# O and dQ of a grouped-query attention step from 64x256 instead of 32x128 matmul blocks

## The chip, the core and the metric

The kernel runs on one NeuronCore of a Trainium2 chip. The time is the device time of one execution in microseconds. A core has TensorE (PE: matmuls and transposes, which write PSUM), VectorE (DVE), ScalarE (ACT) and GpSimd (POOL) for elementwise work, and SyncE (SP), on whose queue this kernel issues all its transfers between SBUF and the main memory. Each engine works through its own instructions in order. A matmul takes a stationary operand, loaded by an instruction of its own (PEld in the profile), and streams a moving operand past it, column by column. The array can be split into tiles of fewer stationary columns that work side by side, each writing its own PSUM partitions. GpSimd does not take part in emptying PSUM in this kernel; VectorE and ScalarE do that.

## What is computed

Attention of 4 query positions for 32 query heads over 2048 keys in 4 key heads, for 32 batches with head size 128, and the gradients for q, k and v. Cut to what matters:

```python
def _fwd_reference(q, k, v):            # q (32, 32, 4, 128), k and v (32, 4, 2048, 128)
    k = jnp.repeat(k, rep, axis=1)      # rep = 8 query heads share one key head
    v = jnp.repeat(v, rep, axis=1)
    scores = jnp.einsum("bhqd,bhkd->bhqk", q, k) * scale
    p = _softmax(scores, axis=-1)
    return jnp.einsum("bhqk,bhkd->bhqd", p, v)

_out, _vjp = jax.vjp(_f, q, k, v)
_grads = _vjp(grad_out)                 # dq, dk, dv
```

For one batch, the 8 query heads times 4 positions of one key head are 32 rows, so the four key heads fill the 128 partitions: rows 32h to 32h+31 belong to key head h. With E the unnormalised softmax numerators (128 rows, 2048 keys), r the reciprocal of their row sums and G the output's gradient, the kernel makes

- O = r E V and dQ = r scale dS K, in which each group of 32 rows is multiplied by its own head's V or K;
- delta = the row sums of O times G, dS = E (G V^T - delta);
- dV = E^T (r G) and dK = dS^T (r scale Q).

## The kernel before

K and V of a batch come as two rows of SBUF each, one for two heads. Twenty such rows ("slots") hold loads and results alike: a result row is gathered in a slot and stored from there. The row for heads 2 and 3 of dV carries O behind its 4096 columns, that of dK carries dQ; the loaded rows of K carry q and the output's gradient in the same place.

The instructions stand in an order written out by hand. `PLAN` is one long text in which four characters are one unit: a letter for the kind of unit (`NAMES`, lines 23 to 26), its part, the engine, PSUM bank or slot that it uses, and a tile number. `emit` (line 214) turns a unit into instructions. The framework only adds the waits that the data and the buffers need, so all engines follow the order of this text.

The units of the change, by letter: `p`/`q` transpose E and empty PSUM; `r` (O) and `y` (DQ) are the products in question, in two halves each (lines 279 to 289); `s` (Oe) and `z` (DQe) scale them from PSUM into the result row (lines 290 to 296); `t` (DL) makes delta (lines 297 to 300); `u` (DP) and `v` (DS) are G V^T and dS in two halves; `A` and `C` are the matmuls of dV and dK, `B` and `D` empty them; `m`, `n` and `o` are three small GpSimd instructions (r G, r scale Q, r scale); `E` and `F` store dV and dK; `a` and `b` load K and V.

In a product of O, the stationary operand is a 128x32 piece of transposed E: 128 keys, the 32 rows of head h. The moving operand is 128 keys by 128 columns of V of the same head. Four such matmuls, one for each head, stand in four tiles of 32 stationary columns and write PSUM partitions 32h to 32h+31, columns 0 to 127 of one bank. Eight groups of four make one half, so O has 64 matmuls in a batch and dQ as many. dQ of one batch is made while the next batch's O is in work: in the order, O of batch b is followed by the two halves of dQ of batch b-1.

The order of one later batch around the change, with the units named in the text:

```
r020r1-0 s0D0 t0D0 o0-0 A640B6A0 A760B7D0 y030 C500D5A0 y1-0 z0D0 F180 u040 v0D0 ...
```

Delta follows directly on O's scaling, then come two parts of dV, dQ's two halves with a part of dK between them, dQ's scaling, the store of dK's second row with dQ in it, and then DP and dS, which reads delta.

A load or a store waits for its data, for its slot and for the transfer that last used its completion semaphore; all wait in SP's one queue.

Of the kernel before, what the change touches and what calls it, by code (L numbers as in the profile page):

```python
# [10 lines left out]
BF16 = mybir.dt.bfloat16  # L11
ACT = mybir.ActivationFunctionType
ALU = mybir.AluOpType

P = 128
NH = 4
ROW = 2 * 16 * P
# [36 lines left out]
    "f3D0A260B2A0E0c0u100v1D0g732h7A0e627f6A0n0-0C040D0D0C160D1A0C300D3D0a1g0g634h6A0g226h2A0i041i1-0j0D0C220D2A0g300"
    "h3A0e410f4A0w120x1A0g131h1D0k0A0g403h4D0g015h0D0C420D4D0w001x0A0l0D0e012f0A0C640D6A0F0i0C760D7D0e703f7A0e514p020"
    "q0A0f5D0b160p131q1D0m0-0A340B3A0A060B0D0A100B1A0a040r020r1-0s0D0t0D0o0-0A640B6A0A760B7D0y030C500D5A0y1-0z0D0F130"
    "u041v0D0g520h5A0A560B5A0E150b0e0A400B4D0e231f2A0e125f1A0c040d0D0e356f3D0A260B2A0E020u100v1D0g731h7A0e627f6A0n0-0"
    "C040D0D0C160D1A0C300D3D0a1b0g635h6A0g226h2A0i040i1-0j0D0C220D2A0g300h3A0e411f4A0w121x1A0g132h1D0k0A0g403h4D0g014"
    "h0D0C420D4D0w000x0A0l0D0e012f0A0C640D6A0F000C760D7D0e705f7A0e516p020q0A0f5D0b1a0p131q1D0m0-0A340B3A0A060B0D0A100"
    "B1A0a030r020r1-0s0D0t0D0o0-0A640B6A0A760B7D0y030C500D5A0y1-0z0D0F170u040v0D0g520h5A0A560B5A0E1i0b0f0A400B4D0e230"  # L60
    "f2A0e123f1A0c040d0D0e354f3D0A260B2A0E0c0u100v1D0g732h7A0e627f6A0n0-0C040D0D0C160D1A0C300D3D0a190g634h6A0g226h2A0"
    "i041i1-0j0D0C220D2A0g300h3A0e410f4A0w120x1A0g131h1D0k0A0g403h4D0g015h0D0C420D4D0w001x0A0l0D0e012f0A0C640D6A0F0h0"
    "C760D7D0e703f7A0e514p020q0A0f5D0b150p131q1D0m0-0A340B3A0A060B0D0A100B1A0a070r020r1-0s0D0t0D0o0-0A640B6A0A760B7D0"
    "y030C500D5A0y1-0z0D0F1j0u041v0D0g520h5A0A560B5A0E100b060A400B4D0e231f2A0e125f1A0c040d0D0e356f3D0A260B2A0E020u100"
    "v1D0g731h7A0e627f6A0n0-0C040D0D0C160D1A0C300D3D0a1e0g635h6A0g226h2A0i040i1-0j0D0C220D2A0g300h3A0e411f4A0w121x1A0"
    "g132h1D0k0A0g403h4D0g014h0D0C420D4D0w000x0A0l0D0e012f0A0C640D6A0F010C760D7D0e705f7A0e516p020q0A0f5D0b1i0p131q1D0"
    "m0-0A340B3A0A060B0D0A100B1A0a0j0r020r1-0s0D0t0D0o0-0A640B6A0A760B7D0y030C500D5A0y1-0z0D0F180u040v0D0g520h5A0A560"
# [3 lines left out]
    "t0D0o0-0A640B6A0A760B7D0y030C500D5A0y1-0z0D0F1g0u041v0D0g520h5A0A560B5A0E110b050A400B4D0e231f2A0e125f1A0c040d0D0"  # L71
    "e356f3D0A260B2A0E020u100v1D0g731h7A0e627f6A0n0-0C040D0D0C160D1A0C300D3D0a160g635h6A0g226h2A0i040i1-0j0D0C220D2A0"
    "g300h3A0e411f4A0w121x1A0g132h1D0k0A0g403h4D0g014h0D0C420D4D0w000x0A0l0D0e012f0A0C640D6A0F040C760D7D0e705f7A0e516"
    "p020q0A0f5D0b1h0p131q1D0m0-0A340B3A0A060B0D0A100B1A0a0g0r020r1-0s0D0t0D0o0-0A640B6A0A760B7D0y030C500D5A0y1-0z0D0"
    "F1b0u040v0D0g520h5A0A560B5A0E1d0b0i0A400B4D0e230f2A0e123f1A0c040d0D0e354f3D0A260B2A0E0c0u100v1D0g732h7A0e627f6A0"
    "n0-0C040D0D0C160D1A0C300D3D0a1a0g634h6A0g226h2A0i041i1-0j0D0C220D2A0g300h3A0e410f4A0w120x1A0g131h1D0k0A0g403h4D0"
    "g015h0D0C420D4D0w001x0A0l0D0e012f0A0C640D6A0F030C760D7D0e703f7A0e514p020q0A0f5D0b110p131q1D0m0-0A340B3A0A060B0D0"
    "A100B1A0a0b0r020r1-0s0D0t0D0o0-0A640B6A0A760B7D0y030C500D5A0y1-0z0D0F190u041v0D0g520h5A0A560B5A0E140b000A400B4D0"
    "e231f2A0e125f1A0c040d0D0e356f3D0A260B2A0E020u100v1D0g731h7A0e627f6A0n0-0C040D0D0C160D1A0C300D3D0a150g635h6A0g226"
    "h2A0i040i1-0j0D0C220D2A0g300h3A0e411f4A0w121x1A0g132h1D0k0A0g403h4D0g014h0D0C420D4D0w000x0A0l0D0e012f0A0C640D6A0"  # L80
    "F070C760D7D0e705f7A0e516p020q0A0f5D0b1d0p131q1D0m0-0A340B3A0A060B0D0A100B1A0a090r020r1-0s0D0t0D0o0-0A640B6A0A760"
    "B7D0y030C500D5A0y1-0z0D0F1e0u040v0D0g520h5A0A560B5A0E130b0h0A400B4D0e230f2A0e123f1A0c040d0D0e354f3D0A260B2A0E0c0"
    "u100v1D0g732h7A0e627f6A0n0-0C040D0D0C160D1A0C300D3D0a1i0g634h6A0g226h2A0i041i1-0j0D0C220D2A0g300h3A0e410f4A0w120"
    "x1A0g131h1D0k0A0g403h4D0g015h0D0C420D4D0w001x0A0l0D0e012f0A0C640D6A0F0f0C760D7D0e703f7A0e514p020q0A0f5D0b140p131"
    "q1D0m0-0A340B3A0A060B0D0A100B1A0a0e0r020r1-0s0D0t0D0o0-0A640B6A0A760B7D0y030C500D5A0y1-0z0D0F1j0u041v0D0g520h5A0"
# [3 lines left out]
    "s0D0t0D0o0-0A640B6A0A760B7D0y030C500D5A0y1-0z0D0F180u040v0D0g520h5A0A560B5A0E1f0b0d0A400B4D0e230f2A0e123f1A0c040"  # L89
    "d0D0e354f3D0A260B2A0E0c0u100v1D0g732h7A0e627f6A0n0-0C040D0D0C160D1A0C300D3D0a1h0g634h6A0g226h2A0i041i1-0j0D0C220"  # L90
    "D2A0g300h3A0e410f4A0w120x1A0g131h1D0k0A0g403h4D0g015h0D0C420D4D0w001x0A0l0D0e012f0A0C640D6A0F0a0C760D7D0e703f7A0"
    "e514p020q0A0f5D0b170p131q1D0m0-0A340B3A0A060B0D0A100B1A0a080r020r1-0s0D0t0D0o0-0A640B6A0A760B7D0y030C500D5A0y1-0"
    "z0D0F1g0u041v0D0g520h5A0A560B5A0E160b040A400B4D0e231f2A0e125f1A0c040d0D0e356f3D0A260B2A0E020u100v1D0g731h7A0e627"
    "f6A0n0-0C040D0D0C160D1A0C300D3D0a110g635h6A0g226h2A0i040i1-0j0D0C220D2A0g300h3A0e411f4A0w121x1A0g132h1D0k0A0g403"
    "h4D0g014h0D0C420D4D0w000x0A0l0D0e012f0A0C640D6A0F050C760D7D0e705f7A0e516p020q0A0f5D0b1f0p131q1D0m0-0A340B3A0A060"
    "B0D0A100B1A0a0g0r020r1-0s0D0t0D0o0-0A640B6A0A760B7D0y030C500D5A0y1-0z0D0F1b0u040v0D0g520h5A0A560B5A0E1a0b030A400"
    "B4D0e230f2A0e123f1A0c040d0D0e354f3D0A260B2A0E0c0u100v1D0g732h7A0e627f6A0n0-0C040D0D0C160D1A0C300D3D0a1d0g634h6A0"
    "g226h2A0i041i1-0j0D0C220D2A0g300h3A0e410f4A0w120x1A0g131h1D0k0A0g403h4D0g015h0D0C420D4D0w001x0A0l0D0e012f0A0C640"
    "D6A0F090C760D7D0e703f7A0e514p020q0A0f5D0b160p131q1D0m0-0A340B3A0A060B0D0A100B1A0a0b0r020r1-0s0D0t0D0o0-0A640B6A0"
    "A760B7D0y030C500D5A0y1-0z0D0F1i0u041v0D0g520h5A0A560B5A0E150b070A400B4D0e231f2A0e125f1A0c040d0D0e356f3D0A260B2A0"  # L100
# [6 lines left out]
    "r1-0s0D0t0D0o0-0A640B6A0A760B7D0y030C500D5A0y1-0z0D0F1j0u041v0D0g520h5A0A560B5A0E100b060A400B4D0e231f2A0e125f1A0"  # L107
    "c040d0D0e356f3D0A260B2A0E020u100v1D0g731h7A0e627f6A0n0-0C040D0D0C160D1A0C300D3D0a170g635h6A0g226h2A0i040i1-0j0D0"
    "C220D2A0g300h3A0e411f4A0w121x1A0g132h1D0k0A0g403h4D0g014h0D0C420D4D0w000x0A0l0D0e012f0A0C640D6A0F010C760D7D0e705"
    "f7A0e516p020q0A0f5D0b190p131q1D0m0-0A340B3A0A060B0D0A100B1A0a0j0r020r1-0s0D0t0D0o0-0A640B6A0A760B7D0y030C500D5A0"  # L110
    "y1-0z0D0F180u040v0D0g520h5A0A560B5A0E1h0b0a0A400B4D0e230f2A0e123f1A0c040d0D0e354f3D0A260B2A0E0c0u100v1D0g732h7A0"
    "e627f6A0n0-0C040D0D0C160D1A0C300D3D0a1f0g634h6A0g226h2A0i041i1-0j0D0C220D2A0g300h3A0e410f4A0w120x1A0g131h1D0k0A0"
    "g403h4D0g015h0D0C420D4D0w001x0A0l0D0e012f0A0C640D6A0F0d0C760D7D0e703f7A0e514p020q0A0f5D0b100p131q1D0m0-0A340B3A0"
    "A060B0D0A100B1A0a080r020r1-0s0D0t0D0o0-0A640B6A0A760B7D0y030C500D5A0y1-0z0D0F1g0u041v0D0g520h5A0A560B5A0E110b050"
    "A400B4D0e231f2A0e125f1A0c040d0D0e356f3D0A260B2A0E020u100v1D0g731h7A0e627f6A0n0-0C040D0D0C160D1A0C300D3D0a160g635"
    "h6A0g226h2A0i040i1-0j0D0C220D2A0g300h3A0e411f4A0w121x1A0g132h1D0k0A0g403h4D0g014h0D0C420D4D0w000x0A0l0D0e012f0A0"
    "C640D6A0F040C760D7D0e705f7A0e516p020q0A0f5D0b1h0p131q1D0m0-0A340B3A0A060B0D0A100B1A0a0g0r020r1-0s0D0t0D0o0-0A640"
    "B6A0A760B7D0y030C500D5A0y1-0z0D0F1b0u040v0D0g520h5A0A560B5A0E1d0b090A400B4D0e230f2A0e123f1A0c040d0D0e354f3D0A260"
    "B2A0E0c0u100v1D0g732h7A0e627f6A0n0-0C040D0D0C160D1A0C300D3D0a1a0g634h6A0g226h2A0i041i1-0j0D0C220D2A0g300h3A0e410"
    "f4A0w120x1A0g131h1D0k0A0g403h4D0g015h0D0C420D4D0w001x0A0l0D0e012f0A0C640D6A0F030C760D7D0e703f7A0e514p020q0A0f5D0"  # L120
    "b110p131q1D0m0-0A340B3A0A060B0D0A100B1A0a0b0r020r1-0s0D0t0D0o0-0A640B6A0A760B7D0y030C500D5A0y1-0z0D0F1i0u041v0D0"
# [3 lines left out]
    "r020r1-0s0D0t0D0o0-0A640B6A0A760B7D0y030C500D5A0y1-0z0D0F1e0u040v0D0g520h5A0A560B5A0E130b0h0A400B4D0e230f2A0e123"  # L125
    "f1A0c040d0D0e354f3D0A260B2A0E0c0u100v1D0g732h7A0e627f6A0n0-0C040D0D0C160D1A0C300D3D0a190g634h6A0g226h2A0i041i1-0"
    "j0D0C220D2A0g300h3A0e410f4A0w120x1A0g131h1D0k0A0g403h4D0g015h0D0C420D4D0w001x0A0l0D0e012f0A0C640D6A0F0f0C760D7D0"
    "e703f7A0e514p020q0A0f5D0b140p131q1D0m0-0A340B3A0A060B0D0A100B1A0a0e0r020r1-0s0D0t0D0o0-0A640B6A0A760B7D0y030C500"
    "D5A0y1-0z0D0F1j0u041v0D0g520h5A0A560B5A0E170b010A400B4D0e231f2A0e125f1A0c040d0D0e356f3D0A260B2A0E020u100v1D0g731"
    "h7A0e627f6A0n0-0C040D0D0C160D1A0C300D3D0a100g635h6A0g226h2A0i040i1-0j0D0C220D2A0g300h3A0e411f4A0w121x1A0g132h1D0"  # L130
    "k0A0g403h4D0g014h0D0C420D4D0w000x0A0l0D0e012f0A0C640D6A0F060C760D7D0e705f7A0e516p020q0A0f5D0b130p131q1D0m0-0A340"
    "B3A0A060B0D0A100B1A0a0j0r020r1-0o0-0s0D0t0D0A640B6A0A760B7D0y030C500D5A0y1-0z0D0F180u040v0D0g520h5A0A560B5A0E1f0"
    "b0d0A400B4D0e230f2A0e123f1A0c040d0D0e354f3D0A260B2A0E0c0u100v1D0g732h7A0e627f6A0n0-0C040D0D0C160D1A0C300D3D0a1h0"
    "g634h6A0g226h2A0i041i1-0j0D0C220D2A0g300h3A0e410f4A0w120x1A0g131h1D0k0A0g403h4D0g015h0D0C420D4D0w001x0A0l0D0e012"
    "f0A0C640D6A0F0a0C760D7D0e703f7A0e514p020q0A0f5D0p131q1D0b170m0-0A340B3A0A060B0D0A100B1A0r020r1-0s0D0t0D0o0-0A640"
    "B6A0A760B7D0y030C500D5A0y1-0z0D0F1g0u041v0D0g520h5A0A560B5A0E160b040A400B4D0e231f2A0e125f1A0c040d0D0e356f3D0A260"
    "B2A0E020u100v1D0g731h7A0e627f6A0n0-0C040D0D0C160D1A0C300D3D0g635h6A0g226h2A0i040i1-0j0D0C220D2A0g300h3A0e411f4A0"
    "w121x1A0g132h1D0k0A0g403h4D0g014h0D0C420D4D0w000x0A0l0D0e012f0A0C640D6A0F050C760D7D0e705f7A0e516p020q0A0f5D0p131"
    "q1D0m0-0A340B3A0A060B0D0A100B1A0r020r1-0s0D0t0D0o0-0A640B6A0A760B7D0y030C500D5A0y1-0z0D0F1b0u040v0D0g520h5A0A560"
    "B5A0E180A400B4D0e230f2A0e123f1A0c040d0D0e354f3D0A260B2A0E010u100v1D0g732h7A0e627f6A0n0-0C040D0D0C160D1A0C300D3D0"  # L140
    "g634h6A0g226h2A0i041i1-0j0D0C220D2A0g300h3A0w110x1A0g121h1A0k0A0g433h4D0g005h0D0C420D4D0w011x0A0l0D0C640D6A0F0f0"
    "C760D7D0p000q0A0p111q1D0m0-0A320B3A0A040B0D0A160B1A0r000r1-0s0D0t0D0o0-0A620B6A0A740B7D0y010C560D5A0y1-0z0D0F1c0"
    "u021v0D0g500h5A0A440A560B5A0E130B4D0A200B2A0E0a0u120v1D0n0-0C060D0D0C140D1A0C300D3A0C220D2A0w141x1A0C400D4D0w050"
# [17 lines left out]
def kernel(  # L161
# [11 lines left out]
    nc = tc.nc  # L173
# [14 lines left out]
    junk = const_pool.tile([P, D], BF16, name="junk")  # L188
# [13 lines left out]
    def bank(u, n=1):  # L202
        return psum[:, QW * int(u.where):QW * (int(u.where) + n)]
# [10 lines left out]
    def emit(u):  # L214
        b, name, i = u.b, u.name, u.part
        t = T[b]
        if name in ("LK", "LV"):
            x = slots[int(u.where, 36)]
            for h in range(2):
                t[name[1], 2 * i + h] = x[:, Sk * h:Sk * h + Sk]  # L220
            if name == "LK":
                t["q" if i == 0 else "go"] = x[:, ROW:LONG]
# [56 lines left out]
        elif name in ("O", "DQ"):  # L279
            if i == 0:  # L280
                t[name] = bank(u)[:, 0:D]
            xt, x = ("ET", "V") if name == "O" else ("DT", "K")
            left = t[xt, i][:].rearrange("p (j q e) -> p j q e", q=P, e=2)
            for c in range(8):
                j, odd = divmod(c, 2)
                for h, r in enumerate(rows):
                    right = t[x, h].rearrange("p (j d e) -> p j d e", d=D, e=2)
                    nc.tensor.matmul(t[name][r, :], lhsT=left[:, j, r, odd], rhs=right[:, 4 * i + j, :, odd],  # L288
                                     start=(i == 0 and c == 0), stop=(i == 1 and c == 7), tile_position=(0, 32 * h))
        elif name in ("Oe", "DQe"):  # L290
            x, by, to = ("o", "rinv", "DV") if name == "Oe" else ("dq", "rs", "DK")
            t[x] = t[to, "out", 1][:, ROW:LONG]
            if u.where == "A":
                nc.scalar.activation(out=t[x], in_=t[name[:-1]], func=ACT.Copy, scale=t[by][:])
            else:
                nc.vector.tensor_scalar(out=t[x], in0=t[name[:-1]], scalar1=t[by][:], scalar2=None, op0=ALU.mult)  # L296
        elif name == "DL":
            t["dl"] = sm_pool.tile([P, 1], FP32, name="delta")
            nc.vector.tensor_tensor_reduce(out=junk[:], in0=t["o"], in1=t["go"], scale=1.0, scalar=0.0,
                                           op0=ALU.mult, op1=ALU.add, accum_out=t["dl"][:])  # L300
        elif name == "DS":
# [60 lines left out]
```

## Time and profile before

| | us |
|---|---|
| three runs | 672.08, 670.65, 673.27 |
| median | 672.08 |
| span of the profiled execution | 671.1 |
| ACT busy in it | 569.6 |
| DVE busy in it | 572.0 |
| O's matmuls (L288, reading transposed E), busy | 36.1 |
| dQ's matmuls (L288, reading transposed dS), busy | 43.5 |
| L296, two of 128x128 a batch: mean | 0.34 and 0.35 |

The profile is of one execution. A page of it gives the busy time of each engine, the span in 40 slices with the share of time in which the transfers' sixteen engines were busy, the chain of work that ended last, and groups of equal instructions. A row of a timeline has the start and the length in us, the engine, the line of the kernel, the operation, and what it writes from what; a number in brackets is the time for which the engine had been idle before it, with what ended that. A row of a table of stretches has the stretch, its length, the busy time of each engine with the number of its instructions, the granted clock of TensorE as a share of the full one, the transfers' busy share and their rate. The busy time of matmuls that run side by side, or follow each other in the pipeline, is counted once, and each one's own length has the way through the array in it, so the pace of matmuls is read from the starts.

### The profile page before, as it was taken

What the parts mean: (1) busy time and instruction counts of PE and PEld (TensorE: products, weight loads), DVE (VectorE), ACT (ScalarE), POOL (GpSimd) and SP (SyncE); (2) the same over time, 40 slices, a digit from 0 to 9 for tenths busy, and PEclk for the clock granted to TensorE, in tenths of its full rate; (3) what the DMA queues carried; (4) which work ended last, traced back from release to release, by engine and by line L of the source; (5) the groups of instructions that cost most, each with busy time, mean ns of one, the idle gap of its engine ahead of it and who ended that gap; (6) DMA issues with size and microseconds to landing.
All of it is one profiled execution on the core that took longest, in us unless ns stands there. A gap on an engine that the chain in (4) does not pass through costs nothing.

```text
span 671.1 us, 20678 instructions
## 1 busy us (share of the span) xinstructions
PE 607.9 (91%) x8768; PEld 401.4 (60%) x8768; DVE 572.0 (85%) x736; ACT 569.6 (85%) x802; POOL 39.0 (6%) x102
## 2 busy tenths in 40 slices
PE   6998999999998999988998989988999989898993
PEld 5665566666665666655655655655655666565651
DVE  1988799999997999988888989887888979896994
ACT  4997899999997999888888989887888979886894
POOL 0000000000000000000000000000000000000000
PEclk9999999999998999999999999998999989998997
DMA  9999999999999999999999999999999999999867
GB/s 354 417 424 423 419 381 423 423 423 423 423 426 424 424 423 424 424 425 426 414 420 425 413 417 421 414 422 424 396 388 408 417 424 424 404 421 423 347 258 322
DMA packets 37533, 273.97 MB, mean 408 GB/s; under 512 B 4160, under 2 KB 4160, under 8 KB 5184
## 3 DMA queue, kind: packets, MB, share of 16 engines
q1 hardware_dynamic: 37440, 272.65, 98.2%
q8 instruction: 69, 1.13, 0.6%
q14 instruction: 24, 0.20, 0.1%
HBM read 136.31 MB, written 136.31 MB: 406 GB/s over the span
## 4 chain that ended last, share of the span: by engine, by line
DMA 50%; PE 37%; DVE 4%; ACT 4%; issue 3%; SPq 0%; POOL 0%; DVEq 0%; ACTq 0%; POOLq 0%
DMA row<-in_k_dram 50%; PE psum L241 19%; PE psum L310 8%; PE psum L288 5%; PE psum L255 5%; ACT row L316 3%; DVE vt_sb L209 2%; DVE ds_sb L303 1%; DVE row L316 0%; DVE e_sb L260 0%; ACT e_sb L264 0%; PE psum L230 0%; SPq L226 0%; ACT dt_sb L207 0%; DVE row L296 0%
## 5 line engine op out<-in xcount | busy, mean ns | idle before, releaser
L241 PE MATMUL psum<-ident,row 128*128 128x128 f32 x2048 | 290.1, 284 | 28.4 <-DMA row<-in_k_dram 21.5
L316 ACT CAST row<-psum 128x1024 bf16<-128x1024 f32 x292 | 289.2, 1023 | 30.9 <-PE psum L310 29.1
L241 PEld LDWEIGHTS psum<-ident,row 128*128 128x128 f32 x2048 | 224.7, 143 | 94.8 <-issue 32.0
L316 DVE CAST row<-psum 128x1024 bf16<-128x1024 f32 x220 | 264.9, 1217 | 5.7 <-PE psum L310 2.9
L207 ACT COPY kt_sb<-psum 128x512 f32<-128x512 f32 x190 | 110.2, 598 | 20.6 <-PE psum L241 20.4
L207 ACT COPY vt_sb<-psum 128x512 f32<-128x512 f32 x160 | 92.0, 602 | 35.3 <-PE psum L241 34.6
L303 DVE SCALAR_TENSOR_TENSOR ds_sb<-psum,delta,e_sb 128x1024 bf16<-128x1024 f32 x64 | 82.1, 1283 | 13.4 <-PE psum L255 9.0
L310 PE MATMUL psum<-ds_sb,qp_sb 32*128 32x512 bf16 x512 | 76.9, 383 | 3.4 <-ACT row L316 1.0
L260 DVE TENSOR_SCALAR_CACHE_REDUCE e_sb<-psum 128x2048 bf16<-128x2048 f32 x32 | 73.3, 2292 | 5.7 <-PE psum L255 5.7
L310 PE MATMUL psum<-e_sb,dop_sb 32*128 32x512 bf16 x512 | 68.8, 388 | 2.5 <-issue 1.0
L209 DVE COPY kt_sb<-psum 128x1024 bf16<-128x1024 bf16 x66 | 45.0, 685 | 28.4 <-PE psum L241 27.8
L209 DVE COPY vt_sb<-psum 128x1024 bf16<-128x1024 bf16 x96 | 60.7, 684 | 10.0 <-PE psum L241 9.8
L264 ACT ACTIVATE e_sb<-psum,m 128x2048 bf16<-128x2048 f32 x32 | 64.0, 2001 | 0.2 <-DVE e_sb L260 0.2
L271 POOL TENSOR_SCALAR dop_sb<-row,rinv 128x128 bf16<-128x128 bf16 x32 | 19.3, 603 | 605.3 <-DVE rinv L268 530.3
L241 PE MATMUL psum<-ident,ds_sb 128*128 128x128 f32 x256 | 41.8, 286 | 9.6 <-DVE vt_sb L209 7.0
L288 PE MATMUL psum<-row,dt_sb 128*32 128x128 bf16 x2048 | 43.5, 222 | 6.2 <-issue 5.6
L310 PEld LDWEIGHTS <-qp_sb 32*128 32x128 bf16 x512 | 19.4, 91 | 46.1 <-issue 42.6
L255 PE MATMUL psum<-vt_sb,qdt_sb 128*32 128x512 bf16 x512 | 40.7, 388 | 4.6 <-issue 4.5
L288 PEld LDWEIGHTS <-dt_sb 128*32 128x32 bf16 x2048 | 30.8, 95 | 22.0 <-issue 21.1
L241 PEld LDWEIGHTS psum<-ident,ds_sb 128*128 128x128 f32 x256 | 26.9, 140 | 27.2 <-DVE vt_sb L209 16.4
L207 ACT COPY dt_sb<-psum 128x512 f32<-128x512 f32 x63 | 38.4, 611 | 1.0 <-PE psum L241 0.9
L288 PEld LDWEIGHTS <-et_sb 128*32 128x32 bf16 x2048 | 30.4, 95 | 13.8 <-ACT et_sb L207 11.3
(29 smaller groups left out, 310.1 us busy)
## 6 DMA issues: line engine op xcount, KB each, us to landing
out_dram<-row SPq DMA_DIRECT2D x64, 1056.0 KB, 20.1
out_dram<-row SPq DMA_DIRECT2D x64, 1024.0 KB, 20.4
row<-in_k_dram SPq DMA_DIRECT2D x62, 1056.0 KB, 18.1
row<-in_v_dram SPq DMA_DIRECT2D x62, 1024.0 KB, 20.5
row<-in_v_dram SPq DMA_DIRECT2D x4, 512.0 KB, 9.4
row<-in_k_dram SPq DMA_DIRECT2D x2, 544.0 KB, 5.3
row<-in_k_dram SPq DMA_DIRECT2D x2, 512.0 KB, 4.4
```

What stands on the lines that cost most here:

```text
L207: nc.scalar.copy(out=out.bitcast(FP32), in_=in_)
L209: nc.vector.tensor_copy(out=out, in_=in_.bitcast(BF16))
L241: nc.tensor.transpose(out=ps[:, P * j:P * j + P], in_=src[:, 4 * half + j, :], identity=ident32[:])
L255: nc.tensor.matmul(out[r, QW * w:QW * w + QW], lhsT=t["qdt"][:, P * side + 32 * h:P * side + 32 * h + 32], rhs=t[x, NH * i + h][:, QW * w: ...
L260: nc.vector.tensor_scalar(out=t["e"][:], in0=t["S"], scalar1=-scale, scalar2=None, op0=ALU.mult, op1=ALU.min, accum_out=t["m"][:])
L264: nc.scalar.activation(out=t["e"][:], in_=t["S"], func=ACT.Exp, bias=t["m"][:], scale=scale, accum_out=t["l"][:])
L271: nc.gpsimd.tensor_scalar(out=t["dop"][:], in0=t["go"], scalar1=t["rinv"][:], scalar2=None, op0=ALU.mult)
L288: nc.tensor.matmul(t[name][r, :], lhsT=left[:, j, r, odd], rhs=right[:, 4 * i + j, :, odd], start=(i == 0 and c == 0), stop=(i == 1 and c ...
L303: nc.vector.scalar_tensor_tensor(out=t["ds"][:, w], in0=t["DP", i], scalar=t["dl"][:], in1=t["e"][:, w], op0=ALU.subtract, op1=ALU.mult)
L310: nc.tensor.matmul(acc[:, QW * (h % 2):QW * (h % 2) + QW], lhsT=t[still][rows[h], :], rhs=t[moving][rows[h], QW * i:QW * i + QW], start=Tr ...
L316: copy(out=heads_of(t[name[:2], "out", g])[:, :, QW * i:QW * i + QW], in_=t[name[:2], i, g].rearrange("p (h c) -> p h c", h=2))
```

## The change

O and dQ are made for two heads at a time. The stationary operand is 128x64, the rows of heads 2g and 2g+1; the moving operand is 128 keys by 256 columns, the same keys and columns of V or K of both heads, which lie in one row of SBUF. Two such matmuls stand in two tiles of 64 stationary columns. Of the 64x256 block that each makes, the two 32x128 blocks on the diagonal are the result; the other two, rows of one head times the other head's V or K, are not used. A half of O or dQ is 16 matmuls instead of 32, so a batch has 64 instead of 128 for both, and the PSUM block is 128x256.

VectorE scales the whole 128x256 block into one SBUF tile, `both`, which has one buffer, and GpSimd copies the four diagonal blocks from there to the result row. In the last batch VectorE scales the four blocks directly into the row. The tile `junk`, into which delta's instruction wrote products that nobody reads, is gone; that output goes into `both` as well. In the order, delta (`t`) is moved from behind O's scaling to behind the first half of DP (`u`), in every batch. Nothing else in the order changes.

```diff
-    ... r020r1-0s0D0t0D0o0-0A640B6A0A760B7D0y030C500D5A0y1-0z0D0F180u040v0D0 ...
+    ... r020r1-0s0D0o0-0A640B6A0A760B7D0y030C500D5A0y1-0z0D0F180u040t0D0v0D0 ...
...
-    junk = const_pool.tile([P, D], BF16, name="junk")
...
+            t[name[1], "pair", i] = x[:, 0:ROW]
...
-                t[name] = bank(u)[:, 0:D]
+                t[name] = bank(u)[:, 0:2 * D]
...
-                for h, r in enumerate(rows):
-                    right = t[x, h].rearrange("p (j d e) -> p j d e", d=D, e=2)
-                    nc.tensor.matmul(t[name][r, :], lhsT=left[:, j, r, odd], rhs=right[:, 4 * i + j, :, odd],
-                                     start=(i == 0 and c == 0), stop=(i == 1 and c == 7), tile_position=(0, 32 * h))
+                for g in range(2):
+                    r = slice(64 * g, 64 * g + 64)
+                    right = t[x, "pair", g].rearrange("p (h j d e) -> p h j d e", h=2, d=D, e=2)
+                    nc.tensor.matmul(t[name][r, :], lhsT=left[:, j, r, odd], rhs=right[:, :, 4 * i + j, :, odd],
+                                     start=(i == 0 and c == 0), stop=(i == 1 and c == 7), tile_position=(0, 64 * g))
...
-            if u.where == "A":
-                nc.scalar.activation(out=t[x], in_=t[name[:-1]], func=ACT.Copy, scale=t[by][:])
+            mine = [(r, slice(D * (h % 2), D * (h % 2) + D)) for h, r in enumerate(rows)]
+            both = sm_pool.tile([P, 2 * D], BF16, name="both", bufs=1)
+            if b == B - 1:
+                for r, c in mine:
+                    nc.vector.tensor_scalar(out=t[x][r, :], in0=t[name[:-1]][r, c], scalar1=t[by][r, :], scalar2=None,
+                                            op0=ALU.mult)
             else:
-                nc.vector.tensor_scalar(out=t[x], in0=t[name[:-1]], scalar1=t[by][:], scalar2=None, op0=ALU.mult)
+                nc.vector.tensor_scalar(out=both[:], in0=t[name[:-1]], scalar1=t[by][:], scalar2=None, op0=ALU.mult)
+                for r, c in mine:
+                    nc.gpsimd.tensor_copy(out=t[x][r, :], in_=both[r, c])
         elif name == "DL":
+            spare = sm_pool.tile([P, 2 * D], BF16, name="both", bufs=1)
             t["dl"] = sm_pool.tile([P, 1], FP32, name="delta")
-            nc.vector.tensor_tensor_reduce(out=junk[:], in0=t["o"], in1=t["go"], scale=1.0, scalar=0.0,
+            nc.vector.tensor_tensor_reduce(out=spare[:, 0:D], in0=t["o"], in1=t["go"], scale=1.0, scalar=0.0,
                                            op0=ALU.mult, op1=ALU.add, accum_out=t["dl"][:])
```

## The prediction

> **What bounds the kernel now.** I read the page first, then stretches of single batches, then the timeline of one batch engine by engine.
>
> ```profile
> span 671.1 us, 20678 instructions
> PE 607.9 (91%) x8768; PEld 401.4 (60%) x8768; DVE 572.0 (85%) x736; ACT 569.6 (85%) x802; POOL 39.0 (6%) x102
> DMA  9999999999999999999999999999999999999867
> q1 hardware_dynamic: 37440, 272.65, 98.2%
> ```
>
> The transfers are busy nearly throughout, PE almost as much. Which of the two is the bound changes on the way. The stretches below run from one batch's first K transposes on PE to the next one's.
>
> ```profile
> core 0: us, PE busy (x) PEld busy (x) DVE busy (x) ACT busy (x) POOL busy (x), PEclk, DMA share, GB/s
> 138.27:157.12 18.85, 18.49 (x275) 12.21 (x276) 17.84 (x24) 17.54 (x26) 1.20 (x3) 1.00 1.01 425
> 195.74:218.10 22.36, 20.13 (x276) 12.95 (x276) 18.12 (x24) 17.70 (x26) 1.20 (x3) 0.92 1.01 424
> 399.63:420.12 20.49, 18.60 (x274) 12.29 (x274) 17.96 (x24) 17.71 (x25) 1.28 (x5) 1.00 1.01 421
> ```
>
> Until about 255 us a batch takes 18.85 us, with PE busy for 18.49 of them: compute sets the pace, and eats up the loads that had run ahead. From there to 606 us a batch takes 20.5 us for the same work, and the chain of waits is one K load after another: transfers set the pace. So compute has a reserve of 20.5 - 18.85 = 1.65 us a batch and no more. The second row holds a stall of PE of 1.88 us ("issue" in the chain) after which the granted clock was 0.92.
>
> **What the change adds on PE.** One batch's part of it:
>
> ```profile
> 138.27 0.15 DVE L268 RECIPROCAL rinv<-l 128x1 f32<-128x1 f32 x1
> 138.68 0.60 POOL L271 TENSOR_SCALAR dop_sb<-row,rinv 128x128 bf16<-128x128 bf16 x1 [17.48 <-DVE rinv L268]
> ...
> 139.36 0.22 POOL L278 TENSOR_SCALAR rs<-rinv 128x1 f32<-128x1 f32 x1
> ...
> 140.63 1.12 PE L288 MATMUL psum<-row,et_sb 128*32 128x128 bf16 x64
> ...
> 142.31 0.29 DVE L299 CUSTOM_DVE_ANT_0 junk<-row,row 128x128 bf16<-128x128 bf16 x1
> ...
> 142.40 0.65 PE L288 MATMUL psum<-row,dt_sb 128*32 128x128 bf16 x32
> ...
> 143.30 0.66 PE L288 MATMUL psum<-row,dt_sb 128*32 128x128 bf16 x32
> ...
> 143.78 0.61 PE L255 MATMUL psum<-vt_sb,qdt_sb 128*32 128x512 bf16 x8
> 144.11 0.35 DVE L296 TENSOR_SCALAR row<-psum,rs 128x128 bf16<-128x128 f32 x1 [0.36 <-PE psum L288]
> ...
> 144.50 1.28 DVE L303 SCALAR_TENSOR_TENSOR ds_sb<-psum,delta,e_sb 128x1024 bf16<-128x1024 f32 x1
> ```
>
> From start to next start O (64 matmuls, sixteen groups of four) held PE for 1.05 us (140.63 to 141.68), the first half of DQ (eight groups) 0.58, the second 0.48, being followed by a product of the same tile shape. O less the first half gives 0.059 us a group of four 128-column matmuls, and 0.11 us for entering the shape. After the change a group is two matmuls of 256 columns. No row shows that shape. Bounds: by instructions alone, half of 0.059, 0.03 us; if the two ran one after the other, both with 256 columns, 0.22. The nearest row is L255, four 32-wide tiles side by side with 512 columns: sixteen took 0.98 us, eight 0.54, so 0.22 us a group, 0.11 for 256 columns if two tiles run side by side as four do. I take 0.11, columns rather than instructions. O becomes 16 x 0.11 + 0.11 = 1.87 us (+0.82); each half of DQ 8 x 0.11 + 0.11 = 0.99 (+0.41, and +0.51 for the second, which now leaves into another shape). Sum +1.74 us a batch; some 0.17 of it covers a wait that the DV pair behind O has now for a cast, so **+1.57 us**. PE's own loop becomes 18.85 + 1.57 = 20.4 us: the reserve is gone by this alone. By the bounds the same terms give -0.8 and +5.1 us; the upper one goes against L255's row and is left to rival 4.
>
> The Trainium skill speaks against this edit too: "TensorEngine Tiling (Array Packing)", section Theoretical Speedup, gives up to 4x for a small dimension of 32 and up to 2x for 64. And "TensorE: Matmul & The Clock Gate", section Back-to-back issue gap, gives N/2.4 + 2.5 ns: 56 ns at 128 columns, where the row has 59, and an estimate of 109 at 256; the sum by it would be the same to 0.1 us.
>
> **What it adds on VectorE and GpSimd.** L296 reads 256 columns instead of 128. The cast of 1024 columns (1.217 us) against 0.35 us for 128 gives 0.97 ns a column, so +0.12 us, twice. Then GpSimd copies four 32x128 blocks, and VectorE's delta (L299) is moved: from right behind O's scaling to behind DQ's scaling and the DP matmuls. The four copies of O have time: they follow O's scaling by 2 us and more before anything reads them.
>
> The copies of DQ have not. The delta's throwaway output lies in the same single buffer ("both", bufs=1) that DQ's scaling has just written and that GpSimd is still reading. In the changed program's order the delta stands next behind DQ's scaling on VectorE and waits for GpSimd's count after DQ's last copy. So a new wait appears each batch: DQ's scaling, hand-over to GpSimd, four copies, hand-over back, delta, DS. Queued behind it on VectorE stand DS, the casts that free PSUM, the Q and K evacuations and the maximum; PE, ACT and the stores wait for those. Prices: hand-over 138.42 to 138.68, 0.26 us. Four copies: below, instructions that overlap as the page's four constant memsets do at the start (30 ns from one start to the next), each as the 0.20 us of the 128x128 memset, 0.3; above, four of L271 at 0.60 with the 0.08 between L271's end and L278's start, 2.7. The nearest row is the affine select on 128x128 bf16 (0.29 us, SBUF to SBUF): end to end four would be 1.16, and since the later three wait for nothing, I take 1.1. Back 0.06. Wait: **1.4 us**, bounds 0.6 and 3.0. Then delta and its accumulator read, 0.36 us, formerly in a gap, now in front of DS.
>
> **The loop on VectorE.** From the end of the E^T evacuation (140.89) to DQ's scaling, VectorE waits for PE: 3.22 us before. After: O ends 0.99 to 1.61 us after that evacuation, then DV matmuls 0.55, DQ 0.99, DK 0.32, DQ 0.88, and 0.33 to the scaling's start: 4.2 to 4.7, I take 4.45. Scaling 0.47, wait 1.42, delta 0.36. The rest of the round, DS at 144.50 to the next E^T evacuation's end at 159.74, is 15.24 us of gapless work but for 0.48 of waits on PE, some of which go: 15.0. Sum 4.45 + 0.47 + 1.42 + 0.36 + 15.0 = **21.7 us a batch**; bounds 20.4 and 23.8. That is over the 20.5 of the transfers, so these cease to be the bound and cover nothing.
>
> **The sum.** The first batch's block of K and E transposes starts at 18.92 us, the thirty-second's at 648.6, so 31 rounds; 22.5 us are left behind them. After: 18.9 + 31 x 21.7 = 691.6. Tail: 22.5 + 2.9 for the longer round (21.7 less 18.85) + 1.6 for the last batch, where four scalings at 0.35 stand for one: 1.05 us for DQ, half of it for O, which has cover. That is 27. Stalls like the one at 195.74 cost 11 us in the first eleven rounds before (218.4 less 11 x 18.85), but PE now idles about 1.3 us a round and takes most of them: 5. Sum 723.6 span. The profiled span, 671.1, stands 1.0 below the median of 672.08, so **724.5 us**, 8% slower.
>
> **Rivals.** (1) The copies overlap on GpSimd and the wait is at its lower bound of 0.6; then VectorE's round is about 20.7, PE's 20.4, and the time is 18.9 + 31 x 20.7 + 5 + 26 + 1 = 692. For: the memsets' overlap; against: a record of 0.22 us for a single element (L278). (2) The transfers still cover everything: the round stays under 20.5, and only the tail grows, by two to three rounds of 1 us: 672 + 3 = 675. For: 98.2% queue share; it needs PE's price near instructions alone. (3) Faster: half as many instructions shorten PE by 0.8 us a round and remove the "issue" stalls. The bytes stay, 272.65 MB at 424 GB/s are 643 us, so it can win only in the tail, some three rounds and two stalls' remains: about 667. Against it: columns, not instructions, fit the rows. (4) Slower still: PE's waits grow to the 1.9 us after which the clock was 0.92; the throttled work then adds up to 22.36 - 18.85 - 1.88 = 1.6 us a round, 23.3 in all: 18.9 + 31 x 23.3 + 28 + 5 + 1 = 775. It decides once one gap of PE passes the 1.5 us that PE waits for a K load in each round now, at clock 1.00. Two 64-wide tiles that run one after the other would give as much: PE's round 18.85 + 5.1 = 24.0.
>
> **How the numbers follow.** Main case 0.62, its own range 703 to 750; (1) 0.18; (2) 0.06; (3) 0.04; (4) 0.10. The time is that of the main case. The range takes in (1) and the greater price of copies: 688 to 752. A measurement of this kernel can tell 0.5%, 3.4 us, from no change. Faster by more is (3), 0.04; within it half of (2), 0.03; slower the rest, 0.93.
>
> **What would show it.** On VectorE an idle time before the delta, put down to GpSimd, of about 1.4 us in each round; rounds of 21 to 22 us from end to end, alike before and after 255 us; a DMA share that falls from 1.01 to about 0.95 in them; 32 matmuls of O in about 1.87 us. It would be wrong if the copies took 0.3 us together, if the delta waited only for O's copies, or if a pair of 64x256 matmuls started every 0.06 us.

## The result, and the profile after

| | before | after |
|---|---|---|
| median, us | 672.18 (5 runs, 670.65 to 673.88) | 725.96 (5 runs, 725.79 to 727.71) |
| ratio to before, 95% interval | | 1.0807 [1.0789, 1.0824] |
| span of the profiled execution, us | 671.1 | 725.9 |

The change costs 54 us, 8.1%. The page of the changed kernel, cut to the lines that answer to those of before, its line of shares by engine in the chain of waits, and its group for the new copies:

```profile
span 725.9 us, 16845 instructions
PE 655.5 (90%) x6720; PEld 442.1 (61%) x6720; DVE 580.3 (80%) x742; ACT 574.1 (79%) x802; POOL 113.0 (16%) x350
...
DMA  9999999999999999999999999999999999999547
...
q1 hardware_dynamic: 37440, 272.65, 96.1%
...
PE 46%; issue 14%; DVE 13%; ACT 9%; POOL 9%; DMA 7%; DVEq 0%; POOLq 0%; SPq 0%; ACTq 0%
...
L303 POOL COPY row<-both 32x128 bf16<-32x128 bf16 x248 | 70.9, 286 | 178.9 <-DVE both L301 171.3
```

PE does 2048 matmuls fewer and is busy for 48 us more. The transfers still look busy throughout, but the chain has left them: K loads alone held 50% of it before, all transfers together hold 7% now, and GpSimd, at 0% before, holds 9%. The stretches of one batch, one ordinary and one that is not (from the E transposes of one batch to those of the next):

```profile
core 0: us, PE busy (x) PEld busy (x) DVE busy (x) ACT busy (x) POOL busy (x), PEclk, DMA share, GB/s
325.43:347.34 21.91, 20.22 (x211) 13.69 (x212) 18.12 (x24) 17.79 (x26) 3.58 (x11) 1.00 1.00 389
501.51:525.08 23.57, 21.57 (x212) 14.30 (x211) 18.19 (x24) 18.01 (x26) 3.57 (x12) 0.93 1.00 386
```

Of the 31 rounds 24, counted from delta to delta, take 21.9 us, early and late alike. No engine is busy for the whole of it: the round is a loop of waits. Where it goes through is seen in the timeline of one batch:

```profile
414.98 0.69 DVE L208 COPY et_sb<-psum 128x1024 bf16<-128x1024 bf16 x1
...
415.41 2.02 PE L289 MATMUL psum<-row,et_sb 128*64 128x256 bf16 x32
...
417.36 0.39 PE L318 MATMUL psum<-e_sb,dop_sb 32*128 32x512 bf16 x4
...
417.68 1.10 PE L289 MATMUL psum<-row,dt_sb 128*64 128x256 bf16 x16
...
418.72 0.39 PE L318 MATMUL psum<-ds_sb,qp_sb 32*128 32x512 bf16 x2
...
419.03 1.11 PE L289 MATMUL psum<-row,dt_sb 128*64 128x256 bf16 x16
...
420.07 0.62 PE L255 MATMUL psum<-vt_sb,qdt_sb 128*32 128x512 bf16 x8
420.24 0.48 DVE L301 TENSOR_SCALAR both<-psum,rs 128x256 bf16<-128x256 f32 x1 [1.09 <-PE psum L289]
...
420.79 1.27 POOL L303 COPY row<-both 32x128 bf16<-32x128 bf16 x4 [1.13 <-DVE both L301]
...
422.09 0.29 DVE L307 CUSTOM_DVE_ANT_0 both<-row,row 128x128 bf16<-128x128 bf16 x1 [1.37 <-POOL row L303]
...
422.52 1.28 DVE L311 SCALAR_TENSOR_TENSOR ds_sb<-psum,delta,e_sb 128x1024 bf16<-128x1024 f32 x1
...
423.86 0.27 PE L230 MATMUL psum<-ident,row 128*128 128x128 bf16 x2 [1.24 <-DVE ds_sb L311]
...
436.87 0.69 DVE L208 COPY et_sb<-psum 128x1024 bf16<-128x1024 bf16 x1
```

Read from the E^T evacuation's end (415.67): VectorE has two casts and O's scaling to do and else waits for PE until 420.24, scales dQ, stands idle for 1.37 us while GpSimd copies, makes delta, starts DS at 422.52, and works on, with no pause longer than 0.2 us, to the end of the next E^T evacuation at 437.56. PE in turn stands for 1.24 us before the Q transposes, which DS releases. In the kernel before, the two E^T evacuations between which the prediction reads the same loop are these:

```profile
140.20 0.69 DVE L209 COPY et_sb<-psum 128x1024 bf16<-128x1024 bf16 x1
...
159.05 0.69 DVE L209 COPY et_sb<-psum 128x1024 bf16<-128x1024 bf16 x1
```

The waits view puts one line under each of the two idle times (total, times, longest):

```profile
DVE both L307 <- POOL row L303: 41.5, 32, 1.4
...
PE psum L230 <- DVE ds_sb L311: 36.9, 30, 1.6
```

### The profile page after: what moved, and what is told of

Same layout as the page of the kernel before. It is cut to its first block, busy times and chain, and to the rows that moved or that the text cites. A ratio compares the mean times of both kernels' runs of the same rounds, so it can differ in the third digit from the quotient of the medians.

```text
span 725.9 us, 16845 instructions
## 1 busy us (share of the span) xinstructions
PE 655.5 (90%) x6720; PEld 442.1 (61%) x6720; DVE 580.3 (80%) x742; ACT 574.1 (79%) x802; POOL 113.0 (16%) x350
## 4 chain that ended last, share of the span: by engine, by line
PE 46%; issue 14%; DVE 13%; ACT 9%; POOL 9%; DMA 7%; DVEq 0%; POOLq 0%; SPq 0%; ACTq 0%
PE psum L241 25%; PE psum L318 9%; POOL row L303 8%; ACT row L324 8%; PE psum L255 7%; PE psum L289 6%; DMA out_dram<-row 5%; DVE row L324 5%; DVE vt_sb L208 4%; DMA row<-in_k_dram 2%; DVE both L301 2%; DVE ds_sb L311 1%; DVE both L307 1%; POOL rs L278 1%; ACT e_sb L264 1%
## 5 line engine op out<-in xcount | busy, mean ns | idle before, releaser
L324 ACT CAST row<-psum 128x1024 bf16<-128x1024 f32 x292 | 292.7, 1016 | 87.7 <-PE psum L318 85.7
L241 PE MATMUL psum<-ident,row 128*128 128x128 f32 x2048 | 286.2, 281 | 8.9 <-DMA row<-in_k_dram 7.8
L303 POOL COPY row<-both 32x128 bf16<-32x128 bf16 x248 | 70.9, 286 | 178.9 <-DVE both L301 171.3
L271 POOL TENSOR_SCALAR dop_sb<-row,rinv 128x128 bf16<-128x128 bf16 x32 | 19.3, 602 | 409.7 <-PE psum L318 378.9
L289 PE MATMUL psum<-row,dt_sb 128*64 128x256 bf16 x1024 | 71.9, 282 | 0.1
L289 PE MATMUL psum<-row,et_sb 128*64 128x256 bf16 x1024 | 64.8, 277 | 0.0
L289 PEld LDWEIGHTS <-et_sb 128*64 128x64 bf16 x1024 | 54.7, 108 | 14.6 <-ACT et_sb L206 11.7
L289 PEld LDWEIGHTS <-dt_sb 128*64 128x64 bf16 x1024 | 52.5, 110 | 16.6 <-issue 14.4
L318 PE MATMUL psum<-e_sb,dop_sb 32*128 32x512 bf16 x512 | 57.8, 383 | 0.4 <-ACT vt_sb L206 0.4
```

The lines of the kernel that those rows point to most:

```text
L241: nc.tensor.transpose(out=ps[:, P * j:P * j + P], in_=src[:, 4 * half + j, :], identity=ident32[:])
L271: nc.gpsimd.tensor_scalar(out=t["dop"][:], in0=t["go"], scalar1=t["rinv"][:], scalar2=None, op0=ALU.mult)
L303: nc.gpsimd.tensor_copy(out=t[x][r, :], in_=both[r, c])
L318: nc.tensor.matmul(acc[:, QW * (h % 2):QW * (h % 2) + QW], lhsT=t[still][rows[h], :], rhs=t[moving][rows[h], QW * i:QW * i + QW], start=Tr ...
L324: copy(out=heads_of(t[name[:2], "out", g])[:, :, QW * i:QW * i + QW], in_=t[name[:2], i, g].rearrange("p (h c) -> p h c", h=2))
```

## The experiments

The question is how 54 us come out of parts that each look cheap, and which of the parts could be had without them. The kernel before ran beside each: its medians were 672.53 beside the first four kernels, 672.14 beside the second four, 671.92 beside the last two. Ratios below are to these, with the 95% interval.

**The matmuls alone.** The 64x256 products stay; order, delta and scaling are those of before.

```diff
-            mine = ...
-            both = ...
...
+            nc.vector.tensor_scalar(out=t[x], in0=t[name[:-1]][:, 0:D], scalar1=t[by][:], scalar2=None, op0=ALU.mult)
```

> The 64x256 matmuls alone: order, scaling and delta of the kernel before; the scaling takes columns 0 to 127 of all rows, so the heads 1 and 3 of O and dQ, and what follows from delta, get another head's block. Theory A: PE's round is 18.85 + 1.92 less 0.4, 20.4 us, under the transfers' 20.5, but without a reserve for PE's stalls: 674 to 692. Theory B: 715 or more. Theory D: about 695 to 700.

Measured: 678.59 us, 1.0089 [1.0073, 1.0106]. A stretch of this kernel from delta to delta, early in the run, where before needs 18.85 us a round:

```profile
168.65:189.02 20.37, 20.02 (x214) 13.56 (x212) 17.94 (x24) 17.64 (x26) 1.20 (x3) 1.00 1.01 415
```

PE's round is 20.37, 1.52 more than the 18.85 of before, and it is PE that fills it (20.02 busy). It stays just under the 20.5 us that transfers need, so the whole run loses only 6 us: nearly all of the edit is hidden.

**The copies alone.** The 32x128 products of before, each scaled block copied by GpSimd in four parts, delta in the changed place and with its output in the shared tile; the last batch is scaled directly.

```diff
+                both = sm_pool.tile([P, 2 * D], BF16, name="both", bufs=1)
+                nc.vector.tensor_scalar(out=both[:, 0:D], in0=t[name[:-1]], scalar1=t[by][:], scalar2=None, op0=ALU.mult)
+                for r in rows:
+                    nc.gpsimd.tensor_copy(out=t[x][r, :], in_=both[r, 0:D])
```

> The kernel before, with its 32x128 matmuls, but scaled into the shared buffer, copied to the row by GpSimd in four pieces, and delta in the changed place. So the wait without the wider matmuls. Theory A: VectorE's round becomes 18.85 + 1.4 + 0.4 less some 0.3 of idle time, 20.3 to 20.6, against 20.5 for the transfers: their reserve of 1.65 us a round takes nearly all of it, 673 to 688. Theory B: 672 as before. Theory D (each part costs its share of the 54 us, whatever the transfers do): about 695 to 700.

Measured: 686.53 us, 1.0207 [1.0184, 1.0229], with the wait of 1.37 us before delta in all but the first two batches. The same stretch of this kernel:

```profile
129.87:150.26 20.39, 18.76 (x276) 12.33 (x276) 17.85 (x23) 17.74 (x26) 3.60 (x11) 1.00 1.02 419
...
191.02:213.34 22.32, 19.24 (x273) 12.35 (x273) 17.85 (x24) 17.49 (x25) 3.60 (x11) 0.97 1.01 416
...
479.95:502.76 22.81, 21.69 (x287) 14.05 (x288) 18.02 (x23) 18.41 (x27) 3.61 (x11) 0.93 1.00 405
```

The ordinary round is 20.37 to 20.4 again, now with 18.76 us of PE: this time a wait fills it. Seven rounds behind the fourth are longer, like the two last rows, and hold 8.3 us over 20.37 together; two of them run at a lower clock, and what makes the other five was not settled. Without the seven this kernel would lose about as little as the one before it.

The two experiments give the sum: 18.85 + 1.52 + 1.52 = 21.89, and the changed kernel's round is 21.91. Each edit alone fits into the transfers' reserve of 1.65 us a batch, and both together do not, since they stand one behind the other in VectorE's loop. 6 and 14 us add up to 54 for that reason.

**The wait taken away, in two ways.** Delta's throwaway output gets a tile of its own again (a small tile elsewhere goes from four buffers to two to make room), or the shared tile stays and delta stands ahead of dQ's scaling:

```diff
-            spare = sm_pool.tile([P, 2 * D], BF16, name="both", bufs=1)
...
+            nc.vector.tensor_tensor_reduce(out=junk[:], ...
```

> The changed kernel, but delta's throwaway output has a buffer of its own, so that delta waits for GpSimd's copies of O alone. Theory A (the wait of 1.37 us behind dQ's scaling sits in VectorE's round, and the round of 21.9 us is VectorE's): the wait goes, rounds of about 20.5 us, now PE's and the transfers' too, 680 to 692 us. Theory B (the wider matmuls set the pace, the wait only fills an idle time of VectorE that would be there anyway): 715 us or more. Theory C (copies on GpSimd slow VectorE by being there): close to 726.

```diff
-    ... y1-0z0D0F180u040t0D0v0D0 ...
+    ... y1-0t0D0z0D0F180u040v0D0 ...
```

> The changed kernel, with delta put in front of dQ's scaling in the order instead of behind DP; the shared buffer stays. Delta then waits only for O's copies, which ended 0.9 us before dQ's scaling began. Theory A: as with a buffer of its own, and delta's 0.4 us lie in VectorE's idle time again: rounds of about 20.4 us, 676 to 690. Theory B: 715 or more. Theory C: close to 726.

Measured: 684.22, 1.0169 [1.0149, 1.0189], rounds of 20.4 to 20.5; and 680.63, 1.0120 [1.0105, 1.0136], rounds of 20.33, where delta waits 0.24 us for O's copies. Both keep all matmuls and all copies of the change. So 42 to 45 of its 54 us hang on one buffer dependency and the place where it falls due. The 3.6 us between the two have a candidate in delta's 0.37 us, which only the first still has between dQ's scaling and DS; no run tells this apart from the two buffers taken away.

**The copies, with delta ahead of dQ's scaling, on the matmuls of before.**

```diff
-    ... y1-0z0D0F180u040t0D0v0D0 ...
+    ... y1-0t0D0z0D0F180u040v0D0 ...
```

> The 32x128 matmuls of the kernel before, scaled into the shared buffer and copied by GpSimd in four pieces, with delta in front of dQ's scaling. Theory A: no wait is left on VectorE's round and the copies lie on an engine that is idle 84% of the time: 672, as before, within 3 us. Theory C (copies slow VectorE by being there, or hold up the store of dK): 680 or more.

Measured: 673.22, 1.0012 [1.0001, 1.0024]. Stretches of this kernel, early and late:

```profile
240.87:259.72 18.85, 18.50 (x276) 12.24 (x275) 17.97 (x24) 17.54 (x26) 3.59 (x12) 1.00 1.01 421
...
319.15:339.61 20.46, 18.85 (x276) 12.42 (x275) 18.09 (x23) 17.52 (x25) 3.60 (x11) 1.00 1.01 423
```

These are the rounds of before. Eight copies on GpSimd cost next to nothing as long as no engine is made to wait for them; their work itself, and whatever they share with VectorE, doesn't show.

**The same wait in another place.** The changed kernel with the order of before: delta directly behind O's scaling, so it waits for O's four copies instead of dQ's.

```diff
-    ... s0D0o0-0 ... y1-0z0D0F180u040t0D0v0D0 ...
+    ... s0D0t0D0o0-0 ... y1-0z0D0F180u040v0D0 ...
```

> The changed kernel in the order of the kernel before: delta directly behind O's scaling. It then waits for O's copies, about 1.4 us, in a place where VectorE has 1.1 us of waiting for dQ's matmuls still ahead of it, so that part of it is covered: dQ's scaling about 0.7 us later, DS 1.0 us earlier than in the changed kernel. Theory A: round 20.9 us, 688 to 705. Theory B: 715 or more.

Measured: 689.75, 1.0264 [1.0241, 1.0288], rounds of 20.6. VectorE's rows in the timeline of this kernel:

```profile
419.06 0.48 DVE L301 TENSOR_SCALAR both<-psum,rinv 128x256 bf16<-128x256 f32 x1 [0.82 <-PE psum L289]
420.92 0.29 DVE L307 CUSTOM_DVE_ANT_0 both<-row,row 128x128 bf16<-128x128 bf16 x1 [1.37 <-POOL row L303]
...
421.14 1.22 DVE L324 CAST row<-psum 128x1024 bf16<-128x1024 f32 x1
422.27 0.47 DVE L301 TENSOR_SCALAR both<-psum,rs 128x256 bf16<-128x256 f32 x1
422.66 1.27 DVE L311 SCALAR_TENSOR_TENSOR ds_sb<-psum,delta,e_sb 128x1024 bf16<-128x1024 f32 x1
```

The wait is as long as in the changed kernel, 1.37 us, and costs 36 us less. It falls into a time in which VectorE would have stood idle for dQ's matmuls anyway: the 1.09 us before dQ's scaling of the changed kernel are gone here. Its length does not say what a wait costs.

**The size of the wait.** In the changed kernel, dQ's four copies are replaced by one of 128x128, which takes columns 0 to 127 of all rows, so that dQ holds the wrong head's block in half of them:

```diff
+                if name == "DQe":
+                    nc.gpsimd.tensor_copy(out=t[x], in_=both[:, 0:D])
+                for r, c in mine if name == "Oe" else []:
```

> The changed kernel, with dQ copied by one GpSimd instruction of 128x128 instead of four of 32x128; it takes columns 0 to 127 of all rows, so dQ of heads 1 and 3 is another head's block. Theory A: the wait shrinks from 1.37 to about 0.4 us (one copy at 0.29 with its hand-over), round 20.95 us, 694 to 700. If instead GpSimd's time went by the elements and not by the instructions, the copy would take as long as four, and the time stay at 726.

or one, two or all four of them are made a second time. More copies lengthen the wait, and with it PE's gap: by the theory of the wait alone each round grows by the added wait, by its rival PE's clock joins in.

```diff
-                for r, c in mine:
+                for r, c in mine + (mine[:1] if name == "DQe" else []):
```

> The changed kernel with a fifth copy behind dQ's four. With eight copies the wait was 2.80 us against 1.37, 0.36 us a copy, and the gap of PE before the Q transposes 2.67 us against 1.24; the time rose by 92 us, of which the wait explains 31 x 1.43 = 44. Theory A alone (the wait goes into the round, nothing else): 726 + 31 x 0.36 = 737. Theory F (the granted clock falls once PE's gap passes a bound; here the gap is 1.6 us): 737 if the bound is above 1.6 us, 755 or more if it is below.

> The changed kernel with two more copies behind dQ's four. Theory A alone: 726 + 31 x 0.72 = 748. Theory F: PE's gap is 1.96 us, more than the 1.88 us after which the clock was 0.92 in the kernel before; 765 or more with a clock of about 0.93 in the rounds, 748 if the bound lies above 2 us.

> The changed kernel, with dQ's four copies made twice over, so that delta waits for eight. The copies in the changed kernel's profile took 1.27 us for four. Theory A: the wait grows from 1.37 to about 2.6 us, all of it in the round: 21.9 + 1.25 = 23.15 us, 31 rounds more by 39 us, 762 to 770. Theory F (the fourth rival: once PE's gap before the Q transposes, 1.24 us now, is above 1.5 us, the granted clock falls): above 775, clock in the profile clearly below 0.99. Theory B: within 10 us of 726.

| dQ's copies | median, us | ratio | wait, us | PE's gap before L230, us | rounds, us | their clock |
|---|---|---|---|---|---|---|
| one | 697.21 | 1.0367 [1.0352, 1.0383] | 0.39 | 0.26 | 20.91 | 1.00 |
| four (the change) | 725.96 | 1.0807 [1.0789, 1.0824] | 1.37 | 1.24 | 21.91 | 1.00 |
| five | 745.85 | 1.1099 [1.1058, 1.1139] | 1.72 | 1.59 | 22.25, some 23.60 | 1.00, 0.93 |
| six | 784.85 | 1.1691 [1.1656, 1.1726] | 2.08 | 1.95 | 23.88 | 0.93 |
| eight | 817.94 | 1.2159 [1.2140, 1.2177] | 2.80 | 2.67 | 24.6 to 25.7 | 0.88 to 0.93 |

From one copy to four, wait and round go up alike: 0.98 and 1.00 us. The one copy's row in its timeline, and the delta behind it:

```profile
404.86 0.29 POOL L303 COPY row<-both 128x128 bf16<-128x128 bf16 x1 [1.15 <-DVE both L301]
405.19 0.29 DVE L309 CUSTOM_DVE_ANT_0 both<-row,row 128x128 bf16<-128x128 bf16 x1 [0.39 <-POOL row L303]
```

From four on, something is added. With six, the wait gives 21.9 + 0.7 = 22.6 us a round, and nearly every round takes 1.3 more. Stretches of the kernel with five copies, each from one gap of PE to the next, and a part of the second of them:

```profile
319.72:341.97 22.25, 20.21 (x211) 13.66 (x210) 18.13 (x24) 17.79 (x25) 3.87 (x12) 1.00 1.00 384
341.97:365.57 23.60, 21.60 (x210) 14.56 (x210) 18.12 (x24) 18.08 (x25) 3.86 (x12) 0.93 0.96 363
...
343.90:347.30 3.40, 3.40 (x19) 2.24 (x18) 2.46 (x3) 2.35 (x4) 0.00 (x0) 0.51 1.03 349
```

The two hold the same work and begin with the same gap, as PE's timeline of that kernel has it:

```profile
319.72 0.27 PE L230 MATMUL psum<-ident,row 128*128 128x128 bf16 x2 [1.59 <-DVE ds_sb L311]
...
341.97 0.27 PE L230 MATMUL psum<-ident,row 128*128 128x128 bf16 x2 [1.59 <-DVE ds_sb L311]
```

Behind the first gap the clock stays at 1.00. Behind the second it goes, two microseconds later, to about 0.5 for 3.4 us, and PE's busy time rises from 20.21 to 21.60. Counted over the whole run of this kernel, 5 of 28 gaps of 1.59 to 1.62 us have such a drop behind them, and so has its one gap of 1.96. In the kernel with six copies it is 26 of 28 gaps of 1.95 to 1.99 us; one without and one with:

```profile
96.62:119.42 22.80, 20.40 (x210) 13.78 (x210) 18.11 (x24) 17.79 (x25) 4.15 (x13) 1.00 0.99 374
310.51:334.38 23.87, 21.50 (x211) 14.37 (x210) 18.27 (x24) 17.79 (x25) 4.15 (x13) 0.93 0.97 359
```

These counts are not chances that go with a gap's length. The drops of one run begin whole multiples of 3.413 us apart: with five copies at 275.67, 343.94, 456.58, 524.84, 593.11 and 705.75 us, which is 20, 33, 20, 20 and 33 times that. With six copies the usual round, 23.89 us, is seven times 3.413, so the gap meets this grid at nearly the same place round after round, and the 26 are not 26 separate cases. Nor does the length alone decide: in the kernel before, the clock falls at the end of one gap of 1.51 us, and in the kernel with the copies and delta ahead of dQ's scaling it holds behind one of 1.93. For each, PE's row with the gap in brackets, and a stretch from about the gap's end on:

```profile
544.89 1.94 PE L241 MATMUL psum<-ident,row 128*128 128x128 f32 x8 [1.51 <-DMA row<-in_k_dram]
544.55:547.95 3.40, 3.06 (x15) 3.09 (x16) 0.83 (x2) 0.86 (x3) 0.53 (x2) 0.50 1.02 430
...
470.51 0.66 PE L240 MATMUL psum<-ident,row 128*128 128x128 f32 x4 [1.93 <-DVE ds_sb L306]
470.60:475.00 4.40, 4.40 (x44) 2.96 (x45) 3.08 (x4) 3.74 (x6) 0.00 (x0) 1.00 1.01 413
```

With eight copies the run is 92 us over the changed kernel, of which the longer wait is 30 x 1.43 = 43 (in the first two of the 32 batches delta does not wait for dQ's copies); the other 49 come with a clock of 0.914 over the whole run. Rows from the timeline of that kernel:

```profile
418.02 2.70 POOL L303 COPY row<-both 32x128 bf16<-32x128 bf16 x8 [1.13 <-DVE both L301]
...
422.52 0.37 PE L230 MATMUL psum<-ident,row 128*128 128x128 bf16 x2 [2.67 <-DVE ds_sb L311]
...
424.21 1.04 PE L255 MATMUL psum<-vt_sb,qdt_sb 128*32 128x512 bf16 x8
```

The eight DP matmuls behind the gap take 1.04 us, against 0.62 at 420.07 in the changed kernel. So a longer wait costs its own length alone as long as PE's gap stays short: of the gaps of 1.24 to 1.27 us in the changed kernel none had a drop behind it. In the kernels with more copies the theory that counts the wait alone gave too low a time; for five copies the truth lay between it and the theory of the clock, since only some rounds are hit.

None of the ten kernels is faster than the one before. The lowest that has the 64x256 matmuls and computes all of O and dQ is the one with delta ahead of dQ's scaling, at 680.63.

## Why the prediction came out right, step by step

The prediction was 724.5 us with a range of 688 to 752; 725.96 was measured. By its own steps:

- **The bound.** Right. The reserve of 1.65 us a batch held: each part alone came in at 20.4 us a round and cost 6 and 14 us. In the changed kernel transfers no longer set the pace, early and late rounds being equal.
- **PE's price.** Right. O's matmuls hold PE for 417.36 - 415.41 = 1.95 us, dQ's halves for 1.04 each (forecast 1.87 and 0.99). By the same difference as before, (1.95 - 1.04) / 8 = 0.114 us a pair, forecast 0.11, and 0.13 for entering the shape. The +1.92 of these, less the wait of the DV pair behind O, which fell from 0.72 to 0.32 (417.36 to 417.68) instead of by the 0.17 forecast, give +1.52 (forecast +1.57; PE's round alone 20.37, forecast 20.4). A pair of 64x256 matmuls streams 256 columns where a group of four of 32x128 streams 128 (0.114 against 0.059 us), and half of what it makes is thrown away. The formula that the prediction takes from the Trainium skill ("TensorE: Matmul & The Clock Gate", section Back-to-back issue gap) stands there for an isolated matmul; here a whole group starts every 0.059 or 0.114 us, near its 56 and 109 ns.
- **The hand-over and the copies.** The sum was right by two errors that cancel, which is luck. The hand-over from VectorE to GpSimd took 0.07 us (420.72 to 420.79), not the 0.26 read from L271's start, and four copies 1.27, not 1.1: 0.286 each, end to end with small gaps. Together with 0.03 back, 1.37 against 1.42. So L271's 0.26 is not the price of the way between the engines; what else it held, the runs do not show.
- **VectorE's loop.** Right in each term: 4.57 (forecast 4.45), 0.48 (0.47), 1.37 (1.42), 0.43 (0.36), 15.04 (15.0); 21.9 in all, forecast 21.7. The first term's lower end was given as 4.2, but its parts add up to 4.06; the value taken was not affected.
- **The sum over the batches.** 31 rounds, from the first batch's E transposes (20.34) to the last one's (699.14), are 678.8 us; 672.7 plus 5 of stalls were forecast. The rounds were 0.2 longer each (6.5 us) and the stalls, net of shorter first and last rounds, about nothing (31 x 21.91 = 679.2); here too two errors nearly cancel. The tail of 26.8 is as forecast, 27. The forecast counted its start from the K transposes (18.92 in the kernel before) but the last batch from its E transposes; those of the first batch start at 19.85. So of the 2.3 us by which the span, 725.9, exceeds the forecast 723.6, 0.9 are this slip. Against before, the rounds cost 50.0, the tail 4.3 and the start 0.5.
- **The transfers' share.** Wrong. A fall from 1.01 to about 0.95 was forecast; it stayed at 1.00 while the rate fell from 424 to 389 GB/s. The stores of dK and dV, with a median of some 20 us from issue to landing before, now have 11 to 12. The rate and the landing time showed the slack, the busy share did not.
- **The rivals.** Overlapping copies (1): the copies run end to end, 1.27 us. Full cover by the transfers (2): true of each part alone, not of both. Fewer instructions faster (3): the matmuls alone are slower than before. The clock (4): in the changed kernel the gap is 1.24 us and the clock holds, except in the one round with a gap of 1.59 us, shown above from 501.51, which has a clock of 0.93 and takes 23.57 us. The 1.5 us from which it was to decide is no sharp point: with five copies 23 of 28 gaps of 1.59 to 1.62 us pass at full clock. It also rested on a reading that was too smooth. PE does not wait 1.5 us for a K load in each round of the kernel before; it has six waits of 1.51 to 1.53 us, and the clock fell at one of them, shown above at 544.89. The price of the throttled work, 1.6 us a round in the prediction, is 1.3 with six copies. Two copies more, 0.7 us of gap, double the loss.

## What to carry to other kernels

When a resource off the compute path has a reserve, ask what all edits of a change together take from it: two edits of 1.5 us a round cost 6 and 14 us one at a time, and 54 us together, where they lie in series. A scratch output that nobody reads still orders the engines if it shares a buffer; find what is next in line behind the instruction that reuses it, because a wait of the same 1.37 us cost 36 us more in one place than in another, and moving one instruction took it away. Count columns, not instructions, where a larger block computes parts that are not used.

## What the runs showed of the hardware

- PE's clock drops to half for about 3.4 us after gaps of under 2 us. Of gaps around 1.25 us in the changed kernel none of 28 did it, of gaps around 1.6 us with five copies 5 of 28, of those around 1.96 us with six 26 of 28. The drops of a run lie on a grid of 3.413 us, so the counts hold for these rounds only, and which quantity decides was not settled. The Trainium skill, "TensorE: Matmul & The Clock Gate", tells in Part 1 of a half-rate state and a window of 3.4 us that runs freely: the stretch of 3.40 us at 0.51 and the grid fit, and so does one and the same gap of 1.59 us with and without a drop. Its rule in the section HAM oscillation, no idle gaps of PE over some 3.4 us, does not protect this kernel.
- GpSimd's copy of 32x128 bf16 takes 0.286 us and that of 128x128 0.289: from 32 to 128 partitions, at 128 columns, the price of an instruction doesn't change. Other widths were not run.
